# A weight-landing buffer of its own, fewer x and score tiles, and a later gate for block 2's attention

## The chip, the core and the metric

One core of a Trainium2 chip runs the whole program in one launch. Its engines are TensorE (PE, the matmuls), VectorE (DVE), ScalarE (ACT), GpSimd (POOL) and SyncE (SP, which here issues every DMA). The metric is device microseconds of that core. The kernel before took 1076.9 us (median of 3 runs, 1076.82 to 1080.04).

## The reference

Attention over 4 batches of 8 heads, 576 positions and a head width of 64, in which each query keeps its 32 largest scores; then two feed-forward networks (FFNs) over the 2304 resulting rows of 512.

```python
scores = scale * q @ k.T                       # per head, 576 x 576
kth = partition(scores, -32)[..., -32]
scores = where(scores >= kth, scores, -1e9)
attn = softmax(scores); x = attn @ v           # heads side by side: 2304 x 512
h = maximum(x @ moe_w_in, 0); x = h * h @ moe_w_out         # 512 -> 2048 -> 512
h = maximum(x @ w1, x @ w2, x @ w3); out = h @ moe2_w_out   # 512 -> 768 -> 512
```

The weights come in float64 and are turned into float32 on the chip.

## The kernel before, in words

The rows are cut into six blocks of 384 (`units`, last index but one). For each block and each of four pairs of heads, `attend` runs six jobs of 128 queries against all 576 keys of a head. A job is: two matmul groups of 288 columns into PSUM, copied by ScalarE into a score tile `s`; four MAX8 and three MATCH_REPLACE8 on VectorE, which find the 32nd largest score (tiles `w` and `mx`); three ScalarE passes and one GpSimd pass that make the masked exponentials as two fp16 halves; a transposing DMA (`et`); the product with the values on PE; and a normalisation on GpSimd (`xs`, `xg`). The three row tiles of a pair of heads are then transposed on PE and written into the block's x tile (`xt`), as a high half by ScalarE (L507) and a low half by VectorE (L509). One `xt` tile holds a block's x for all four pairs. A matmul of two float32 numbers is three matmuls of such halves.

`moe(g)` is the FFN of block g. It goes through 28 weight chunks: 16 of the first network, nine of w1, w2 and w3, three of the last matrix. `group` (L630) issues every FFN matmul; a product with x is `a<-xt,wt` or `b<-xt,wt`, the last one is `a<-wt,hh`. x is overwritten in place by the first network's result and is read for the last time by the products with w3.

A weight chunk comes as two halves of 512 KB. The first time, a half is converted (`half_chunk`): the raw float64 words are loaded (L588), ScalarE makes the fraction and the exponent from them (`ot<-xt` by `prelu` and `lw<-xt`), VectorE joins the two (L594, the list `joined` keeps these operations), ScalarE and GpSimd make the two halves of the number, and the result is stored in DRAM (`wsc`). From then on the chunk is only reloaded (L576). There are 56 conversions. The first 36 (EARLY, 18 chunks) are begun two at a time with block 0's attention jobs; the other 20, of the last ten chunks, stand in block 0's FFN and write straight to the weight tiles `wt`, of which there are seven.

The raw words land in a spare x tile: `xt` has three slots, the first is given to `spare`, and its 2 x 4 x 384 words are three landing places of 1024. When the last of the 56 conversions has read them, the slot goes to a block's x.

The order of the work is laid out by the kernel itself. `Plan` keeps a list of operations with engines, assumed durations, priorities and dependences, and places them greedily on five engines with a model of time; a buffer can be opened when a slot of its tag is free, and for all tags but `b` in the order in which the buffers were made. The result is a fixed order for each engine. `plan.after` holds an operation back until another one has been placed: at L719 the attention of blocks 2 to 5 is held until `joined[-9]`, the ninth last join, has begun. The FFNs are not held.

Of the kernel before, what the change touches and what calls it, by code (L numbers as in the profile page):

```python
# [11 lines left out]
F32R = mybir.dt.float32r  # L12
F16 = mybir.dt.float16
BF16 = mybir.dt.bfloat16
U32 = mybir.dt.uint32
# [6 lines left out]
P = 128  # L22
# [244 lines left out]
def kernel(ctx, tc, q, k, v, w_in, w_out, w1, w2, w3, w_out2, out):  # L267
# [3 lines left out]
    KD = DM // P  # L271
    NP = H // 2
# [1 line left out]
    ebias = ESHIFT * float(np.log(2.0))  # L274
    eguard = 1e-9 * 2.0 ** ESHIFT

    nbufs = {"ks": 1, "qs": 1, "vst": 2, "kt": 4, "qt": 1, "vt": 4, "vs": 1, "sm": 2, "sc": 2, "us": 6, "s": 6, "w": 2, "e": 3, "e16": 3,
             "et": 3, "mx": 8, "nb": 8, "rc": 4, "xs": 2, "xr": 2, "xg": 3, "xt": 3,
             "hh": 6, "hl": 6, "r": 2, "m0": 1, "m1": 1, "ot": 3, "cw": 2, "lw": 2, "wt": 7,
             "b": 4, "a": 4}  # L280
    spool = ctx.enter_context(tc.tile_pool(name="sb", bufs=1))
# [3 lines left out]
    plan = Plan(nbufs, {"b"})  # L285

    def buf(tag, shape, dtype=F32):
        return Buf(plan, ppool if tag in ("a", "b") else spool, shape, dtype, tag)
# [4 lines left out]
    def act(prio, n, reads, writes, fn, psum=True, ptr=0):  # L293
        plan.op(ACT, c_act(n, psum, ptr), prio, reads, writes, fn)

    def dve(prio, n, reads, writes, fn, rate=1.0, slack=0.0):
        return plan.op(DVE, c_dve(n, rate), prio, reads, writes, fn, slack=slack)

    def gps(prio, n, reads, writes, fn):
        plan.op(POOL, c_pool(n), prio, reads, writes, fn)  # L300
# [4 lines left out]
    def dma(prio, nbytes, reads, writes, fn, ns=650.0):  # L305
        plan.op(SP, ns, prio, reads, writes, fn, lat=max(nbytes / DBW, 90.0))

    def sub(eng, out_ap, a, b):
        eng.tensor_tensor(out_ap, a, b, op=ALU.subtract)  # L309

    def prelu(out_ap, src, slope, **kw):
        return nc.scalar.activation(out_ap, src, AF.Prelu, alpha=slope, **kw)  # L312
# [28 lines left out]
    NW = max(width)  # L341
    EARLY, PER = 18, 2
    XW = max(len(u[1]) for u in units)
    QW = max(len(u[1]) * 2 * P + (3 * D if u[2] else 0) for u in units)
    spare = buf("xt", [P, 2, KD, NW], F32R)
    work = [(spare, x) for x in range(2 * KD * NW // 1024)]
    xt = {}


# [68 lines left out]
    def attend(i, unit, p):  # L418
# [18 lines left out]
        for j, h in jobs:  # L437
            for _ in range(min(PER if g == 0 else 0, len(ahead))):
                half_chunk(False, *ahead.pop(0))
# [104 lines left out]
    joined = []  # L544
# [13 lines left out]
    def weights(g, n):  # L558

        src = chunk_src[n]  # L560
        a, f = src.shape[1], src.shape[2]
        h = a // 2
        wts = [half_chunk(g > 0 or n < EARLY, n, x) for x in range(2)]

        def view(r, kk):
            return wts[kk // h][:, r].rearrange("p (a f) -> p a f", f=f // 2)[:, kk % h]
        return (lambda kk: wts[kk // h]), view

    def half_chunk(again, n, x):

        src = chunk_src[n]
        h, f = src.shape[1] // 2, src.shape[2]
        src = src[:, x * h:(x + 1) * h, :]
        wt, dst = buf("wt" if again or n >= EARLY else "cw", [P, 2, 512], F32R), scratch[n][x]
        if again:
            dma(W_, P * 4096, [dst], [wt], lambda: nc.sync.dma_start(  # L576
                wt[:].rearrange("p a b -> p (a b)").bitcast(F32), dst[:]))
            return wt
        raw = work[(2 * n + x) % len(work)]
        cv = buf("ot", [P, 512])  # L580

        def bits(t=U32):
            return spare[:].rearrange("p x a b -> p (x a b)")[:, 1024 * raw[1]:1024 * raw[1] + 1024].bitcast(t)

        def word(u):
            return bits().rearrange("p (n u) -> p n u", u=2)[:, :, u]

        dma(W_, P * 4096, [], [raw], lambda: nc.sync.dma_start(bits().rearrange("p (a f) -> p a f", f=f), src))  # L588
        act(C_M, 512, [raw], [cv], lambda: prelu(
            cv[:], word(1).bitcast(F32), -2.0 ** 32, scale=2.0 ** -112), psum=False)  # L590
        lw = buf("lw", [P, 512], U32)
        act(C_M, 512, [raw], [lw], lambda: nc.scalar.activation(  # L592
            lw[:], bits(U8).rearrange("p (n u) -> p n u", u=8)[:, :, 3], AF.Copy, scale=1.0 / 32.0, bias=-15.5 / 32.0), psum=False)
        joined.append(dve(C_D, 512, [cv, lw], [cv], lambda: nc.vector.scalar_tensor_tensor(  # L594
            cv[:].bitcast(U32), cv[:].bitcast(U32), 3, lw[:], op0=ALU.logical_shift_left, op1=ALU.bitwise_or),
            rate=1.7, slack=SL / 2))
        act(C_A, 512, [cv], [(wt, 0)], lambda: nc.scalar.copy(wt[:, 0], cv[:]), psum=False)
        gps(C_P, 512, [cv, (wt, 0)], [(wt, 1)], lambda: sub(nc.gpsimd, wt[:, 1], cv[:], wt[:, 0].bitcast(F32)))
        dma(W_, P * 4096, [wt], [dst], lambda: nc.sync.dma_start(
            dst[:], wt[:].rearrange("p a b -> p (a b)").bitcast(F32)))  # L600
        return wt
# [114 lines left out]

    ahead = [(n, x) for n in range(EARLY) for x in range(2)]
    for i in range(NP * len(units)):
        plan.after = joined[-9] if i >= NP * 3 else None  # L719
        u = units[i // NP]  # L720
        attend(i, u, i % NP)
        if i % NP == NP - 1 and (i // NP == len(units) - 1 or units[i // NP + 1][3] != u[3]):
            plan.after = None
            moe(u[3])
# [66 lines left out]
```

## Time and profile before

| | |
|---|---|
| median of 3 runs | 1076.9 us |
| the profiled execution | 1079.8 us |
| its span, first to last instruction | 1078.0 us |
| busy: PE, DVE, ACT, POOL | 984.3, 818.7, 767.8, 625.3 us |
| attention's maxima on DVE end | about 853 us |
| DMA read from HBM, written | 217.25 MB, 34.08 MB |

Busy time is the time in which an engine has an instruction under way. Matmuls overlap one another, so a matmul's own duration is longer than the time it costs in a row of many. A line in a timeline gives the start, the length, the engine, the source line, the operation and its tiles, written "output<-inputs"; in brackets stands how long the engine was idle before it and who ended that. PEclk is the granted clock of PE as a share of full speed. A DMA share of 1 means that all 16 DMA engines have a transfer under way.

### The profile page before, as it was taken

The numbers are of one execution on the slowest core, as the hardware profiler recorded it, in microseconds if no ns is written. First come the engines' busy times: TensorE is split into PE (matmuls) and PEld (weight loads), VectorE is DVE, ScalarE is ACT, GpSimd is POOL, SyncE is SP. The second block draws the span as 40 slices with busy tenths as digits, with TensorE's granted clock in tenths as the row PEclk, the third lists the DMA queues.
The fourth block names the chain that finished last, engine by engine and source line by source line (L and its number), as shares of the span: only waits on it lengthen the run. The fifth ranks groups of instructions, "written<-read, shape, count | busy, mean of one in ns | idle before, by whom it ended". The sixth has DMA issues, their size and how long they took to land.

```text
span 1078.0 us, 18812 instructions
## 1 busy us (share of the span) xinstructions
PE 984.3 (91%) x6116; PEld 889.7 (83%) x6116; DVE 818.7 (76%) x1736; ACT 767.8 (71%) x1616; POOL 625.3 (58%) x887
## 2 busy tenths in 40 slices
PE   5556576999998999999999999999999999999998
PEld 3333343799897899998999998999998999989997
DVE  5999899899976999999999999999999601100020
ACT  6987788899887889976788868888876742123311
POOL 2666677787787577756467676767565641112210
PEclk9999755799999999999999999999999999999999
DMA  9999899999998999999999999999999986787774
GB/s 306 348 308 251 256 285 332 245 269 231 251 341 318 316 348 283 288 288 256 300 261 266 281 284 274 267 237 262 254 256 280 285 261 237 252 266 262 257 239 147
DMA packets 249697, 295.04 MB, mean 274 GB/s; under 512 B 178944, under 2 KB 182528, under 8 KB 249600
## 3 DMA queue, kind: packets, MB, share of 16 engines
q1 hardware_dynamic: 249600, 293.85, 95.1%
q8 instruction: 48, 0.79, 0.3%
q14 instruction: 49, 0.40, 0.1%
HBM read 217.25 MB, written 34.08 MB: 233 GB/s over the span
## 4 chain that ended last, share of the span: by engine, by line
PE 61%; DVE 13%; ACT 11%; POOL 7%; DMA 4%; issue 3%; SPq 0%; POOLq 0%; ACTq 0%; DVEq 0%
PE a L630 37%; PE b L630 13%; DVE mx L452 7%; DVE w L454 6%; PE b L525 5%; PE b L479 4%; DMA xt<-in_moe_w_in_dram 2%; POOL e L309 2%; ACT s L446 1%; ACT e L312 1%; POOL hl L309 1%; DMA xt<-in_moe_w_dram 1%; ACT lw L592 1%; ACT e L460 1%; ACT ot L312 1%
## 5 line engine op out<-in xcount | busy, mean ns | idle before, releaser
L452 DVE MAX8 mx<-w 128x8 f32<-128x576 f32 x432 | 311.1, 746 | 0.1
L309 POOL TENSOR_TENSOR e<-e,e 128x512 f16<-128x512 f32 (+1 forms) x288 | 211.9, 748 | 108.6 <-ACT e L463 91.3
L630 PE MATMUL a<-xt,wt 128*128 128x384 f32 x1296 | 239.3, 339 | 1.0 <-DVE xt L309 0.9
L630 PE MATMUL b<-xt,wt 128*128 128x384 f32 x1152 | 235.9, 346 | 3.5 <-DMA wt<-wsc 1.9
L630 PE MATMUL a<-hh,wt 128*128 128x384 f32 x768 | 228.8, 346 | 0.0
L630 PEld LDWEIGHTS a<-xt,wt 128*128 128x128 f32 x1296 | 224.1, 188 | 2.2 <-DVE xt L309 1.9
L454 DVE MATCH_REPLACE8 w<-mx,w 128x576 f32<-128x576 f32 x288 | 213.1, 742 | 0.0
L630 PEld LDWEIGHTS b<-xt,wt 128*128 128x128 f32 x1152 | 203.8, 192 | 5.8 <-DMA wt<-wsc 1.9
L525 PE MATMUL b<-kt,qt 128*128 128x288 f32 (+1 forms) x640 | 167.9, 395 | 36.2 <-DMA qt<-in_q_dram 17.8
L309 POOL TENSOR_TENSOR hl<-r,hh 128x384 fp32r<-128x384 f32 x96 | 97.3, 1014 | 126.5 <-ACT hh L656 119.2
L525 PEld LDWEIGHTS b<-kt,qt 128*128 128x128 f32 (+1 forms) x640 | 118.1, 218 | 62.5 <-ACT xs L482 16.4
L630 PEld LDWEIGHTS a<-hh,wt 128*128 128x128 f32 x768 | 142.7, 190 | 2.1 <-issue 1.1
L630 PE MATMUL a<-hl,wt 128*128 128x384 f32 x384 | 131.3, 342 | 4.1 <-POOL hl L309 3.8
L312 ACT ACTIVATE e<-s,mx 128x576 f32<-128x576 f32 x144 | 112.2, 779 | 27.7 <-POOL e L309 16.5
L479 PEld LDWEIGHTS <-et 128*128 128x128 f16 (+1 forms) x1440 | 84.1, 108 | 57.6 <-issue 35.4
L446 ACT ACTIVATE s<-b 128x288 f32<-128x288 f32 x288 | 108.0, 409 | 24.8 <-PE b L525 23.2
L479 PE MATMUL b<-vt,et 128*128 128x129 f16 (+3 forms) x1440 | 101.7, 223 | 25.2 <-DMA et<-e 16.8
L460 ACT ACTIVATE e<-e,nb 128x576 f32<-128x576 f32 x144 | 112.1, 779 | 6.8 <-POOL nb L456 4.8
L452 DVE MAX8 mx<-s 128x8 f32<-128x576 f32 x144 | 107.2, 746 | 10.3 <-ACT s L446 10.3
L454 DVE MATCH_REPLACE8 w<-mx,s 128x576 f32<-128x576 f32 x144 | 106.8, 742 | 0.0
L654 ACT ACTIVATE r<-b 128x384 f32<-128x384 f32 x96 | 47.1, 490 | 79.2 <-PE b L630 76.6
L463 ACT CAST e<-e 128x576 f16<-128x576 f32 x144 | 96.6, 672 | 1.6 <-DMA et<-e 1.3
(62 smaller groups left out, 1194.8 us busy)
## 6 DMA issues: line engine op xcount, KB each, us to landing
wt<-wsc SPq DMA_DIRECT2D x316, 512.0 KB, 4.8
wsc<-cw SPq DMA_DIRECT2D x36, 512.0 KB, 4.9
xt<-in_moe_w_out_dram SPq DMA_DIRECT2D x22, 512.0 KB, 6.3
wsc<-wt SPq DMA_DIRECT2D x20, 512.0 KB, 5.7
xt<-in_moe_w_dram SPq DMA_DIRECT2D x18, 512.0 KB, 5.9
xt<-in_moe_w_in_dram SPq DMA_DIRECT2D x16, 512.0 KB, 5.8
ks<-in_k_dram SPq DMA_DIRECT2D x12, 576.0 KB, 5.9
vst<-in_v_dram SPq DMA_DIRECT2D x16, 320.0 KB, 5.8
```

What stands on the lines that cost most here:

```text
L309: eng.tensor_tensor(out_ap, a, b, op=ALU.subtract)
L312: return nc.scalar.activation(out_ap, src, AF.Prelu, alpha=slope, **kw)
L446: act(A_S, HS, [ps], [(s, f)], lambda s=s, cs=cs, ps=ps: nc.scalar.activation(s[:, cs], ps[:, 0:HS], AF.Copy, scale=escale))
L452: dve(A_X, S, [src], [(mx, r)], lambda src=src, mx=mx, m8=m8: nc.vector.max(out=mx[:, m8], in_=src[:]))
L454: dve(A_X, S + 50, [src, (mx, r)], [w_], lambda src=src, mx=mx, m8=m8, w_=w_: nc.vector.match_replace(out=w_[:], in_to_replace=mx[:, m8], ...
L460: act(A_E, S, [e, nb], [e], lambda nb=nb, e=e: nc.scalar.activation(e[:], e[:], AF.Exp, bias=nb[:], scale=-1.0 / KEEP), psum=False, ptr=1)
L463: act(A_E, S, [e], [(e16, 0)], lambda e=e, e16=e16: nc.scalar.copy(e16[:, S:2 * S], e[:]), psum=False)
L479: nc.tensor.matmul(ps[0:m, 0:wv], et[:, mm_, c0:c1], vt[:, hh, vc, 0:wv], start=x == 0, stop=x == 8)
L525: nc.tensor.matmul(ps[:, 0:HS], a, c, start=m == 0, stop=m == len(seq) - 1)
L592: act(C_M, 512, [raw], [lw], lambda: nc.scalar.activation(lw[:], bits(U8).rearrange("p (n u) -> p n u", u=8)[:, :, 3], AF.Copy, scale=1.0 ...
L630: nc.tensor.matmul(o, x, y, start=first and i == 0 and m == 0, stop=last and i == n - 1 and m == 2)
L654: act(MA, N, [ps], [r], lambda r=r, ps=ps: nc.scalar.activation(r[:, 0:N], ps[:, 0:N], AF.Relu))
```

## The change

Raw weights get four tiles `rw` of their own, of 4 KB in each partition, in place of the three places in the spare x tile. `xt` has two slots in place of three. Score tiles `s` go from six to five, `mx` and `nb` from eight to six. The attention of blocks 2 to 5 is held until the fifth last join in place of the ninth last. Nothing that is computed changes.

```diff
-    nbufs = {... "s": 6, ...
-             "et": 3, "mx": 8, "nb": 8, "rc": 4, "xs": 2, "xr": 2, "xg": 3, "xt": 3,
+    nbufs = {... "s": 5, ...
+             "et": 3, "mx": 6, "nb": 6, "rc": 4, "xs": 2, "xr": 2, "xg": 3, "xt": 2, "rw": 4,
...
-    spare = buf("xt", [P, 2, KD, NW], F32R)
-    work = [(spare, x) for x in range(2 * KD * NW // 1024)]
...
-        raw = work[(2 * n + x) % len(work)]
+        raw = buf("rw", [P, 1024], U32)
         cv = buf("ot", [P, 512])
 
         def bits(t=U32):
-            return spare[:].rearrange("p x a b -> p (x a b)")[:, 1024 * raw[1]:1024 * raw[1] + 1024].bitcast(t)
+            return raw[:].bitcast(t)
...
-        plan.after = joined[-9] if i >= NP * 3 else None
+        plan.after = joined[-5] if i >= NP * 3 else None
```

## Rows read from the trace of the kernel before

**Rows 1.** Page: chain that ended last by line; DMA issues (us to landing).

```profile
PE a L630 37%; PE b L630 13%; DVE mx L452 7%; DVE w L454 6%; PE b L525 5%; PE b L479 4%; DMA xt<-in_moe_w_in_dram 2%; POOL e L309 2%; ACT s L446 1%; ACT e L312 1%; POOL hl L309 1%; DMA xt<-in_moe_w_dram 1%; ACT lw L592 1%; ACT e L460 1%; ACT ot L312 1%
...
xt<-in_moe_w_out_dram SPq DMA_DIRECT2D x22, 512.0 KB, 6.3
```

**Rows 2.** Windows, FFN matmuls alone: stretch, PE and weight-load busy (count), clock, DMA.

```profile
292.00:336.00 44.00, 40.05 (x219) 37.52 (x218) 1.00 1.04 339
...
343.90:349.30 5.40, 0.86 (x2) 0.29 (x1) 0.68 0.49 122
349.30:353.00 3.70, 3.67 (x9) 2.95 (x10) 0.54 0.85 343
353.00:360.30 7.30, 6.57 (x27) 4.61 (x26) 1.00 0.98 328
360.30:362.00 1.70, 0.24 (x2) 0.21 (x2) 1.00 0.98 349
```

**Rows 3.** Chain of waits, 325 to 366 us: start, us, what.

```profile
339.07 2.46 ACT s L446 x9
...
344.57 3.04 POOL kt L309
...
355.07 6.67 DMA wt<-wsc
...
361.79 2.37 PE b L630 x12
```

**Rows 4.** Timeline of VectorE, 319 to 354 us: joins and block 2's first maximum.

```profile
319.41 1.37 DVE L594 SCALAR_TENSOR_TENSOR ot<-ot,lw 128x512 uint32<-128x512 uint32 x1 [2.39 <-ACT lw L592]
...
336.67 0.68 DVE L594 SCALAR_TENSOR_TENSOR ot<-ot,lw 128x512 uint32<-128x512 uint32 x1
338.59 0.76 DVE L452 MAX8 mx<-s 128x8 f32<-128x576 f32 x1 [1.24 <-ACT s L446]
...
353.50 1.67 DVE L594 SCALAR_TENSOR_TENSOR ot<-ot,lw 128x512 uint32<-128x512 uint32 x1
```

**Rows 5.** Timeline of SP round 323 us: block 2's query load, a raw load.

```profile
323.25 0.57 SPq L354 DMA_DIRECT2D qs<-in_q_dram  x1
323.91 0.41 SPq L588 DMA_DIRECT2D xt<-in_moe_w_out_dram  x1
```

**Rows 6.** Timelines: last bias of blocks 2 and 5, their x, block 2's FFN.

```profile
471.48 0.29 POOL L456 TENSOR_SCALAR nb<-mx 128x1 f32<-128x1 f32 x1
...
506.77 0.61 DVE L509 SCALAR_TENSOR_TENSOR xt<-b,us,xt 128x384 fp32r<-128x384 f32 x1
...
514.64 0.69 PE L630 MATMUL b<-xt,wt 128*128 128x384 f32 x3
...
855.56 0.29 POOL L456 TENSOR_SCALAR nb<-mx 128x1 f32<-128x1 f32 x1
...
886.18 0.62 DVE L509 SCALAR_TENSOR_TENSOR xt<-b,us,xt 128x384 fp32r<-128x384 f32 x1 [2.34 <-ACT xt L507]
```

**Rows 7.** Timeline of ScalarE at 334 us: block 2's query cast.

```profile
334.00 0.84 ACT L413 CAST qt<-qs 128x768 fp32r<-128x768 f32 x1
```

**Rows 8.** Waits of the whole span: who, for whom, us, times, longest.

```profile
ACT ot L312 <- POOL cw L309: 9.8, 10, 1.9
```

**Rows 9.** Windows, all engines: PE, PEld, DVE, ACT, POOL busy, clock, DMA share, GB/s.

```profile
300.00:325.00 25.00, 24.62 (x159) 23.79 (x158) 18.32 (x29) 21.20 (x42) 23.52 (x27) 1.00 1.07 346
```

**Rows 10.** Timeline of ScalarE at 795 us: block 5's first x.

```profile
795.62 0.58 ACT L507 ACTIVATE xt<-b,us 128x384 fp32r<-128x384 f32 x1
```

**Rows 11.** Tile xt on PE, 780 to 832 us: durations ns, first and last start.

```profile
L630 PE MATMUL a<-xt,wt x153: 331/336/423, 780.2 to 813.8; 128*128 128x384 f32 x153
```

**Rows 12.** Chain of waits, whole span: PE begins block 5's FFN.

```profile
956.05 4.21 PE b L630 x24
```

**Rows 13.** Timelines at 744 us: a score tile's last reader, the next first maximum.

```profile
743.10 0.79 ACT L312 ACTIVATE e<-s,mx 128x576 f32<-128x576 f32 x1
...
744.88 0.74 DVE L452 MAX8 mx<-s 128x8 f32<-128x576 f32 x1
```

More of the change, by code (lines that the diff above doesn't have):

```diff
@@ L275 @@
     eguard = 1e-9 * 2.0 ** ESHIFT
-    nbufs = {"ks": 1, "qs": 1, "vst": 2, "kt": 4, "qt": 1, "vt": 4, "vs": 1, "sm": 2, "sc": 2, "us": 6, "s": 6, "w": 2, "e": 3, "e16": 3,
-             "et": 3, "mx": 8, "nb": 8, "rc": 4, "xs": 2, "xr": 2, "xg": 3, "xt": 3,
+    nbufs = {"ks": 1, "qs": 1, "vst": 2, "kt": 4, "qt": 1, "vt": 4, "vs": 1, "sm": 2, "sc": 2, "us": 6, "s": 5, "w": 2, "e": 3, "e16": 3,
+             "et": 3, "mx": 6, "nb": 6, "rc": 4, "xs": 2, "xr": 2, "xg": 3, "xt": 2, "rw": 4,
              "hh": 6, "hl": 6, "r": 2, "m0": 1, "m1": 1, "ot": 3, "cw": 2, "lw": 2, "wt": 7,
```

## The prediction, made before the result

> **What bounds the kernel now.** I read the page's chain of waits first: of the chain that ended last, TensorE (PE) on the FFN line L630 has 37% and 13% of the span, and no other line has more than 7% [rows 1]. So a microsecond moves the end only if PE gains or loses it. I then looked for stretches in which PE lacks work after the first block. The table of FFN matmuls by stretch shows one cluster [rows 2]. From 292 to 336 us PE does 219 matmuls in 44 us, 0.18 us each with little else beside them, so it is full. From 343.9 to 349.3 us it does 2. From 349.3 to 353 us it does 9 while the granted clock is 0.54, so nearly all of it at the 1.2 GHz level. From 353 us it does 27 512-wide ones in 6.57 us, 0.23 to 0.24 each. After 360.3 us it has nothing until 361.79 us [rows 2, 3].
>
> The chain of waits inside this hole says why [rows 3]. ScalarE copies scores of block 2 for 2.46 us, GpSimd makes a kt tile of block 2 for 3.04 us, and only then come the last weight halves that block 0's FFN waits for. The second piece is the first reload of block 1's weights: 6.67 us from its issue at 355.07 us to the first matmul at 361.79 us. That issue waits for the last of the 56 conversions, because weight tiles are handed out in a fixed order.
>
> What the hole costs: 5.40 us less two matmuls of 0.23 is 4.9; 3.70 us less nine of 0.23 is 1.6; 361.79 less 360.3 is 1.5. Together 8.0 us, the most that can be won here.
>
> **The change, part by part.** *The wait of block 2.* Nine joins start from 319.41 to 353.50 us on VectorE [rows 4]. The query load of block 2 leaves SP at 323.25 us [rows 5], just behind the ninth last join; VectorE's first maximum of block 2 is at 338.59 us [rows 4], 19.2 us after that join. With the fifth last join as the gate, all of block 2's work (query, key and value loads, casts on ScalarE, kt and qt on GpSimd, scores on PE, and the maxima) is planned after 336.67 us or its new place. It therefore leaves ScalarE and GpSimd free for the last four halves, which today it delays.
>
> When is the fifth last join now? Its raw load leaves SP at 323.91 us [rows 5], 0.66 us behind the query load, once the third landing buffer is free. With a fourth buffer it can leave one conversion earlier, about 3 us, so I put the join at 333.7 us (bounds 331 and 336.7). The last raw load then waits for the buffer of the fifth last half, not the fourth last: issue about 333.5, 6.3 us to landing [rows 1], two ScalarE passes and the join: about 344 us. Today the reload leaves 1.6 us after the last join's start (355.07 less 353.50). So it would leave near 345.5 and land by 352.2 us. PE's last FFN product, 54 matmuls of 0.23 us from 336 us on, ends at about 348.5 us. Of the 8.0 us, up to 3.7 stay as a wait for the reload, and some of them are filled by block 2's scores. I take a gain of **5.0 us**. Bounds: 8.0, and 3.0 if the last four joins keep today's pace of 16.8 us (333.7 + 16.8 + 1.6 + 6.7 = 358.8, 3.0 before 361.8).
>
> *What is late next.* Block 2's attention starts later, and behind it stands the FFN of block 2. VectorE does block 2's jobs back to back after 338.59 us; the last job's bias is at 471.48 us, its x is written from 506.77 to 507.4 us, and PE starts on that x at 514.64 us [rows 6]. The slack is 7.2 us. Of the 19.2 us from gate to first maximum, ScalarE took the query cast only at 334.00 us [rows 7] although the load left at 323.25 us and needs about 6; some 4.6 us of that are conversions in its way. So 14.6 us with them gone: first maximum at 333.7 + 14.6 = 348.3, a delay of 9.7 us (bounds 7 from 331 + 14.6, and 17.3 from 336.67 + 19.2). Four joins of 0.7 us no longer stand between block 2's maxima, which gives back 2.8. The lag from last bias to x is 35.9 us here and 31.2 us in the last block (855.56 to 886.80) [rows 6]; where PE waits for it I take 4 us off. So x is ready at 507.4 + 9.7 - 2.8 - 4 = 510.3 us, against PE being done at 514.64 - 5.0 = 509.6 us. That costs **0.5 us** (bounds 0 and 8.6, below).
>
> *Four landing tiles.* Before 290 us a further buffer buys nothing: ScalarE's first pass already idles for GpSimd's last step on an earlier half [rows 8], so the joined tile is the scarce one there. From 292 to 336 us PE is full, so an earlier conversion is hidden under its matmuls. Value 0 there, its whole worth is in the 3 us above; without that cover it would be worth a few us, and against it stands one more load in a busy queue, 0 to 1.5 us.
>
> A rule speaks against this part. Between 300 and 325 us the DMA engines move 346 GB/s and their share is 1.07 [rows 9]: the queue is full when the extra load would go in. The Trainium skill (DMA: Bandwidth & Descriptors, Queues, rings and completion order) says that an engine takes its descriptors in ring order; so a raw load put ahead of the query load is paid by the query. 0.52 MB at 346 GB/s are 1.5 us, and with them the cost at block 2 would be 2.0 us in place of 0.5, the gain 3.0 in place of 4.5. The sum here leaves it out, since the query is gated behind the load that moves anyway.
>
> *Two x tiles.* Block n+2 writes x only once block n's last product with x is done. Block 5 writes its first x at 795.62 us [rows 10], and block 3 reads its x until 813.8 us [rows 11]: an 18 us wait. Three xg tiles stand ahead of it, and even a shift of the whole block by 18 us puts its x at 905 us against 956.05 us, when PE starts block 5 [rows 6, 12]. Value 0, bounds 0 and a few tenths where PE's order changes.
>
> *Five score tiles, six mx and nb.* In the tightest place that I found, the tile of the fifth job back is released at 743.89 us and the next first maximum is at 744.88 us [rows 13]; a score needs about 2 us from there, so VectorE would lose about 1 us now and then, far behind in time of what PE waits for. Value 0; the bound is 1 us in block 2, where the lead is over 10 us.
>
> **Sum.** -5.0 + 0.5 = -4.5 us. The profiled execution took 1079.8 us (span 1078.0 and 1.8 around it), so it would take 1075.3 us. It lies 2.9 us above the median of the runs shown, 1076.9; from there **1072.4 us**.
>
> **The rivals.** *The hole only moves.* Block 2's first maximum comes about 13 us later (half way between my value and the bound). x is then ready at 515.6 (2 us taken off the lag), PE at 509.6; 6 us, of which one partial product of 1.6 us (nine matmuls that do without the last pair of heads) is filled. -5.0 + 4.4 = -0.6: 1076.3 us. For: the slack is only 7.2 us. Against: the lag can shrink when PE is idle.
>
> *The gate is too late (slower).* One mechanism: the gate join stays at 336.67 us, the path behind it keeps its 19.2 us, and PE runs out of work before block 2's FFN near 512 us. x at 507.4 + 17.3 - 2.8 = 521.9, PE ready at 511.6 with the gain of 3.0; two partial products fill 3.3 us; idle 7.0 and, as after the hole at 343.9, 1.6 us at the lower clock level: 8.6. -3.0 + 8.6 = +5.6: 1082.5 us. It decides from a delay of about 13 us, a first maximum at 352 us. For: from 300 us on the path shares one full DMA queue with the conversions. Against: with the conversions ahead of it, it is alone.
>
> *The whole hole goes and nothing follows*: -8.0, 1069 us. For: no later block is as tight. Against: the reload still needs its 6.67 us.
>
> *Two x tiles hold the last block up*: slower from a delay of 69 us (956.05 less 886.80) on; at 18 us it is free. Its price beyond that is one to one; I set 1083 us.
>
> **How the numbers follow.** Forecast 0.50, the hole only moves 0.20, gate too late 0.20, whole hole gone 0.06, x tiles 0.04. What a measurement of this kernel can tell from no change is about 0.3%, 3.2 us, so faster means under 1073.7 us. The forecast lies only 1.3 us inside that: I count 0.40 of its 0.50 as faster and 0.10 as the same. The moved hole gives 0.16 same and 0.02 to each side. Faster 0.40 + 0.06 + 0.02 = 0.48; same 0.26; slower 0.26. The instruction order of every engine is laid out anew, and a few us either way come with that; so the range goes from 1064 (the whole hole and 5 more) to 1084 us (the late gate and 1.5 more). The forecast's own range is 1069 to 1076.
>
> **What would show it.** Right: no stretch of 5 us between 336 and 365 us in which PE does two FFN matmuls; block 1's first product before 356 us; the last join before 348 us; block 2's first maximum between 345 and 352 us; PE going from block 1 to block 2 near 510 us without a gap of over 2 us and with the clock at its upper level; scores and maxima of later blocks as dense as now. Wrong: the last join still near 353 us (the conversions were not held up by attention); or a gap with a lower clock between 500 and 525 us ahead of the first product of block 2 (late gate); or a gap of PE after 830 us that ends on x (two x tiles).

## The result: slower by 0.6%

The changed kernel takes 1084.2 us (median of 10 runs, 1080.2 to 1089.8) where the kernel before takes 1076.9 us (10 runs, 1074.7 to 1081.6): a ratio of 1.0060, interval 1.0037 to 1.0084. Forecast were 1072.4 us and faster. The two profiled executions took 1082.5 and 1079.8 us: they show 2.7 of the 7.3 us, as the one of before lies 2.9 us above its median and the one of after 1.7 us below.

### The profile page after: what moved, and what is told of

The parts are those of the page before. It is cut to its first block, busy times and chain, and to the rows that moved or that the text cites. A ratio compares the mean times of both kernels' runs of the same rounds, so it can differ in the third digit from the quotient of the medians.

```text
span 1080.7 us, 18818 instructions
## 1 busy us (share of the span) xinstructions
PE 975.4 (90%) x6116; PEld 886.1 (82%) x6116; DVE 819.5 (76%) x1736; ACT 765.3 (71%) x1616; POOL 624.0 (58%) x887
## 4 chain that ended last, share of the span: by engine, by line
PE 73%; ACT 7%; POOL 4%; DVE 4%; issue 3%; DMA 0%; POOLq 0%; ACTq 0%
PE a L628 44%; PE b L628 17%; PE b L523 7%; PE b L477 5%; DVE mx L450 2%; DVE w L452 1%; POOL e L309 1%; ACT s L444 1%; ACT e L458 1%; POOL hl L309 1%; POOL wt L309 1%; ACT e L312 1%; PE b L503 1%; DVE ot L592 1%; ACT lw L590 1%
## 5 line engine op out<-in xcount | busy, mean ns | idle before, releaser
L309 POOL TENSOR_TENSOR e<-e,e 128x512 f16<-128x512 f32 (+1 forms) x288 | 214.1, 755 | 82.0 <-ACT e L461 61.7
L628 PE MATMUL a<-xt,wt 128*128 128x384 f32 x1296 | 242.2, 341 | 0.7 <-DVE xt L309 0.7
L523 PE MATMUL b<-kt,qt 128*128 128x288 f32 (+1 forms) x640 | 162.7, 386 | 32.1 <-DMA qt<-in_q_dram 13.6
L523 PEld LDWEIGHTS b<-kt,qt 128*128 128x128 f32 (+1 forms) x640 | 115.7, 213 | 58.0 <-ACT s L444 14.9
```

The lines of the kernel that those rows point to most:

```text
L523: nc.tensor.matmul(ps[:, 0:HS], a, c, start=m == 0, stop=m == len(seq) - 1)
L628: nc.tensor.matmul(o, x, y, start=first and i == 0 and m == 0, stop=last and i == n - 1 and m == 2)
```

## The profile after

The page: the chain that ended last by line. Lines are two lower than before.

```profile
PE a L628 44%; PE b L628 17%; PE b L523 7%; PE b L477 5%; DVE mx L450 2%; DVE w L452 1%; POOL e L309 1%; ACT s L444 1%; ACT e L458 1%; POOL hl L309 1%; POOL wt L309 1%; ACT e L312 1%; PE b L503 1%; DVE ot L592 1%; ACT lw L590 1%
```

PE on the FFN line now holds 61% of the chain where it held 50% [rows 1]; it is still what a microsecond must be won from. The windows of FFN matmuls that answer to [rows 2]:

```profile
292.00:336.00 44.00, 38.55 (x204) 36.60 (x205) 0.96 1.06 316
...
343.90:349.30 5.40, 4.43 (x20) 3.42 (x19) 1.00 0.82 318
```

The stretch of 5.4 us with two matmuls has 20, and the clock stays at its upper level. But the stretch ahead of it, full before with 219, has 204. The same count over the whole first half says how gain and loss stand. First the kernel before (stretch, PE and weight loads with their counts, clock, DMA):

```profile
0.00:200.00 200.00, 12.18 (x30) 8.41 (x30) 0.81 0.99 296
200.00:225.00 25.00, 18.68 (x87) 16.62 (x87) 0.88 0.98 235
225.00:336.00 111.00, 92.79 (x484) 83.41 (x485) 1.00 1.00 285
336.00:362.00 26.00, 16.03 (x56) 11.13 (x56) 0.87 0.84 303
362.00:515.00 153.00, 129.78 (x657) 113.17 (x656) 1.00 1.06 295
```

Then the changed one:

```profile
0.00:200.00 200.00, 9.81 (x24) 7.01 (x24) 0.74 0.97 285
200.00:225.00 25.00, 16.62 (x89) 15.31 (x90) 1.00 1.08 333
225.00:336.00 111.00, 90.63 (x466) 81.25 (x466) 0.98 1.02 277
336.00:362.00 26.00, 21.28 (x97) 16.83 (x96) 1.00 0.95 346
362.00:515.00 153.00, 127.31 (x638) 111.33 (x636) 0.99 1.02 287
```

Up to 336 us it is 22 matmuls behind (579 against 601), some 4 us at 0.18 us each. In the hole it does 41 more. From 362 to 515 us it does 19 fewer. At 515 us the two are level, 1314 each: the hole was won, and lost ahead of it and behind it. The 2.7 us by which this execution ends later come after that, and most of them inside block 4's FFN: it begins at 829.4 us in both, block 5's 2.2 us later than before (PE, before and after):

```profile
955.88 4.88 PE L630 MATMUL b<-xt,wt 128*128 128x384 f32 x27
```

```profile
958.05 4.87 PE L628 MATMUL b<-xt,wt 128*128 128x384 f32 x27
```

One place behind the hole is at 433.6 us, where PE waits for a low half whose sources stand behind a cast of keys for block 3 and a score copy on ScalarE (the chain of waits there: start, us, what):

```profile
428.19 1.04 ACT kt L363
...
431.11 0.30 ACT s L444
...
432.55 1.01 POOL hl L309
433.55 0.04 issue
433.60 0.62 PE a L628 x2
```

The rows that answer to [rows 4 to 7], out of the timelines of VectorE, SP and ScalarE, and then of GpSimd, PE and VectorE later on:

```profile
332.05 0.70 DVE L592 SCALAR_TENSOR_TENSOR ot<-ot,lw 128x512 uint32<-128x512 uint32 x1 [1.63 <-ACT lw L590]
348.19 0.69 DVE L592 SCALAR_TENSOR_TENSOR ot<-ot,lw 128x512 uint32<-128x512 uint32 x1 [0.49 <-ACT lw L590]
356.13 1.42 DVE L450 MAX8 mx<-s 128x8 f32<-128x576 f32 x2 [1.12 <-ACT s L444]
...
333.40 0.48 SPq L352 DMA_DIRECT2D qs<-in_q_dram  x1
...
348.66 0.83 ACT L411 CAST qt<-qs 128x768 fp32r<-128x768 f32 x1
```

```profile
484.37 0.29 POOL L454 TENSOR_SCALAR nb<-mx 128x1 f32<-128x1 f32 x1
...
515.60 1.66 PE L628 MATMUL b<-xt,wt 128*128 128x384 f32 x8
516.16 0.62 DVE L507 SCALAR_TENSOR_TENSOR xt<-b,us,xt 128x384 fp32r<-128x384 f32 x1
...
896.75 0.62 DVE L507 SCALAR_TENSOR_TENSOR xt<-b,us,xt 128x384 fp32r<-128x384 f32 x1 [2.53 <-ACT xt L505]
```

The fifth last join is at 332.05 us and the last at 348.19 us. The query load leaves at 333.40 us, but ScalarE takes its cast only at 348.66 us, behind all the conversions; block 2's first maximum is at 356.13 us, 24.1 us behind the gate and 17.5 us later than before.

## The experiments

Each ran in five rounds beside the kernel before. The ratio to it is given, because its median moved between 1076.9 and 1080.1 us from one set of runs to the next.

**Which part.** Two theories: the gate is too late (block 2), or the score tiles are too few (front).

```diff
before_gate5:   kernel before,  joined[-9] -> joined[-5]
after_gate9:    kernel after,   joined[-5] -> joined[-9]
before_score5:  kernel before,  "s": 6 -> 5, "mx": 8 -> 6, "nb": 8 -> 6
after_score6:   kernel after,   "s": 5 -> 6, "mx", "nb": 6 -> 8, "rw": 4 -> 3
```

> The kernel before with only the wait of block 2's attention moved from the ninth to the fifth last join; all buffers as before. Late gate (the wait is the cause): block 2's first maximum at 352 to 356 us and a time of 1081 to 1085 us, slower than before by about what the whole change costs (7 us). Score tiles (five of them, and six of mx and nb, are the cause): the hole round 344 us shrinks and nothing is lost ahead of it, 1071 to 1075 us. Landing tiles are the cause: the same, 1071 to 1076 us. As theories on the parts give opposite signs here, this run is the first cut.

> The changed kernel with only the wait put back to the ninth last join; landing, x and score tiles as changed. Late gate: within 2 us of the kernel before, 1075 to 1079 us, with block 2's first maximum near 340 us. Score tiles: the attention of block 0 still ends about 8 us later (x of its last pair of heads near 195 us instead of 187), the hole of 336 to 362 us is back, and the time is 1083 to 1089 us. Landing tiles: also 1082 to 1088 us, told apart from the score tiles by the next run.

> The kernel before with only five score tiles and six mx and nb. Score tiles: the scores of block 0 are written later, x of its last pair of heads comes at 192 to 197 us instead of 187, TensorE loses 2 to 4 us more before 200 us and 2 to 3 us more round 320 us, 1080 to 1084 us. Late gate or landing tiles: x of the last pair at 187 to 189 us, time within 1.5 us of the kernel before.

> The changed kernel with six score tiles and eight mx and nb as before, and three landing tiles of their own instead of four (which is the room that this takes); two x tiles and the wait for the fifth last join stay. Score tiles: block 0's x of the last pair back at 187 to 189 us, the hole smaller than before, 1072 to 1076 us. Late gate: 1081 to 1085 us, with block 2's first maximum at 352 us or later. The two together: about half way, 1077 to 1080 us.

| run | us | ratio, interval |
|---|---|---|
| before_gate5 | 1077.1 | 0.9990, 0.9973 to 1.0006 |
| after_gate9 | 1089.4 | 1.0099, 1.0071 to 1.0127 |
| before_score5 | 1089.9 | 1.0103, 1.0077 to 1.0130 |
| after_score6 | 1076.6 | 0.9989, 0.9972 to 1.0005 |

The late gate fell as the cause of the loss: alone it costs nothing that the runs can tell (0.9990). Both kernels with five score tiles and the ninth last join are 1% slower, after_gate9 just above what was expected. Three landing tiles of their own and two x tiles are worth nothing: after_score6 has them and before_gate5 has not, 0.9989 and 0.9990, and by their traces PE's order is the same in both up to 792 us. The fourth landing tile, and six mx and nb with six score tiles, have no run of their own. But my account of how five tiles cost was wrong: x of block 0's last pair came at 189.4 us (before: 187.0; expected 192 to 197), and the loss was larger than expected.

before_gate5 tests the gate's terms by themselves. Its windows of FFN matmuls, then rows of its timeline (VectorE, PE):

```profile
0.00:355.20 355.20, 137.42 (x655) 118.04 (x656) 0.89 0.99 291
336.00:362.00 26.00, 19.23 (x80) 13.71 (x78) 1.00 0.99 356
505.00:520.00 15.00, 8.77 (x39) 6.87 (x39) 0.89 1.01 260
510.00:515.00 5.00, 2.03 (x6) 1.48 (x7) 0.71 0.79 226
```

```profile
348.25 1.42 DVE L452 MAX8 mx<-s 128x8 f32<-128x576 f32 x2 [1.27 <-ACT s L446]
...
352.37 0.67 DVE L594 SCALAR_TENSOR_TENSOR ot<-ot,lw 128x512 uint32<-128x512 uint32 x1
...
504.04 1.30 PE L630 MATMUL b<-xt,wt 128*128 128x384 f32 x6
...
511.08 0.60 DVE L509 SCALAR_TENSOR_TENSOR xt<-b,us,xt 128x384 fp32r<-128x384 f32 x1
...
515.08 0.52 PE L630 MATMUL a<-hh,wt 128*128 128x384 f32 x1
```

In the hole 80 matmuls stand where 56 stood. A block's FFN has 654 of them; the 655th begins at 355.2 us, where before it began at 361.79 us [rows 3]. So PE leads by 6.6 us after the hole (0.5 us of it from ahead of the hole), and by 10.6 us when it starts block 2 (504.04 us, before 514.64 us [rows 6]). There it runs short: x comes only at 511.08 us, 39 matmuls are done from 505 to 520 us, and the clock is at 0.71 for a part of it. The kernel before has there, and as its first product with block 2's `hh`:

```profile
505.00:520.00 15.00, 12.63 (x55) 9.52 (x54) 1.00 1.10 298
```

```profile
520.31 0.42 PE L630 MATMUL a<-hh,wt 128*128 128x384 f32 x1
```

At that product the lead is 5.2 us, and 3.1 us when block 2 has done 110 matmuls (535.1 us, before 538.2 us). Of 10.6 us, 7.5 are given back at this one hand-over.

**Order or tile.** Five tiles act twice: an instruction waits for a free tile, and the planner, which knows the number, lays out another order. The next run has the order for five tiles (in the traces the same on every engine as before_score5) and six tiles to run in. The two after it hold one score tile back for a part of the time and keep eight mx and nb. Even so five_front has the order of before_score5 up to about 360 us: up to there, six mx and nb add nothing to what five score tiles do to the order. five_later has the order of the kernel before up to about 340 us. The last run moves a constant of the planner.

```diff
order5_tiles6:  before_score5, and the place in memory apart from the planner's count:
-                b.slot = x[1]
+                b.slot = heads[k] % {"s": 6, "mx": 8, "nb": 8}[k[1]] if k[1] in ("s", "mx", "nb") else x[1]
five_front:     kernel before, a tile of "s" taken from the first to the last raw load
+    held = buf("s", [P, S])
+        dma(W_, P * 4096, [held], [raw], ...
five_later:     kernel before, a tile of "s" taken from block 2's first load to the end
jitter_hp:      kernel before
-HP = 1.4
+HP = 1.45
```

> The kernel before whose order is laid out for five score tiles (and six mx and nb), instruction for instruction that of the run with five score tiles, but the tiles of the memory are six (and eight): only the waits for a free tile go. If the wait for a tile costs the 11 us of that run, most of it comes back: 1077 to 1081 us. If the order that five tiles force costs it, the time stays at 1087 to 1091 us.

> The kernel before with one of its six score tiles held back until the last raw weight load, near 330 us: five score tiles for blocks 0 and 1, six after that; its order is that of the run with five score tiles up to about 330 us. There TensorE had lost 5.4 us more than before up to 325 us, and 3.6 us less in the hole behind it. If the front alone pays: 1085 to 1090 us. If the loss is spread over front and later blocks: 1079 to 1083 us, and the cost of this run and the next one add up to about 11 us. If the front is made up for by the hole: 1077 to 1079 us.

> The kernel before with one of its six score tiles held back from block 2's attention to the end: six for blocks 0 and 1, five after that; its order is that of the kernel before up to about 330 us. If only the front pays: within 1.5 us of the kernel before. If the loss is spread: 1082 to 1087 us, with more of TensorE's waits for the hidden low half (hl) of GpSimd in blocks 2 to 5.

> The kernel before, all tiles and the wait as before, with one constant of the planner's time model (the factor on a hop between engines) at 1.45 instead of 1.40: the order is laid out anew for no reason of the work. If a greedy order that is laid out anew is worth several us by chance, 1070 to 1074 or 1082 us and more; if the score tile is the cause as such, within 3 us of the kernel before.

| run | us | ratio, interval |
|---|---|---|
| order5_tiles6 | 1088.9 | 1.0086, 1.0066 to 1.0106 |
| five_front | 1086.7 | 1.0063, 1.0045 to 1.0081 |
| five_later | 1081.9 | 1.0018, 1.0004 to 1.0033 |
| jitter_hp | 1084.1 | 1.0051, 1.0033 to 1.0069 |

The order costs it: without the waits for a tile 1.0086 of 1.0103 is still there, and the intervals do not tell the 0.17% between them from nothing. By five_front and five_later most of it comes with the order of blocks 0 and 1 (0.63% against 0.18%), but the order of five_front behind 360 us is a new one as well, and five_later lies between what its two theories gave. And jitter_hp upset the theory of score tiles: with all six, and no reason in the work at all, a new order cost 0.51%.

**Five tiles, or any new order.**

```diff
six_hop220:   kernel before,  HOP = 180.0 -> 220.0
six_hp135:    kernel before,  HP = 1.4 -> 1.35
five_hp145:   kernel before,  "s": 6 -> 5, HP = 1.4 -> 1.45
five_hp135:   kernel before,  "s": 6 -> 5, HP = 1.4 -> 1.35
after_hp135:  kernel after,   HP = 1.4 -> 1.35
after_hp145:  kernel after,   HP = 1.4 -> 1.45
```

> The kernel before with the planner's time for taking over a freed tile at 220 instead of 180 ns, and nothing else: an order laid out anew with six score tiles. If an order laid out anew costs a few us whatever the tiles (the order of the kernel before is one of the better ones), 0.2 to 0.8% above the kernel before. If the first such run (a hop factor of 1.45, 0.5% slower) was an exception: within 0.2%.

> The kernel before with the planner's hop factor at 1.35 instead of 1.40: a second order laid out anew with six score tiles. Expected as for the run with 220 ns: 0.2 to 0.8% above the kernel before if any new order costs that, within 0.2% if not.

> The kernel before with five score tiles and the hop factor at 1.45. If five tiles as such force a worse order: 0.8 to 1.5% above the kernel before, that is 0.5% or more above the run with six tiles and the same factor. If the loss of the run with five tiles was an unlucky order: 0 to 0.7%, overlapping the runs with six.

> The kernel before with five score tiles and the hop factor at 1.35. As for the factor 1.45: 0.8 to 1.5% above the kernel before if five tiles force a worse order, 0 to 0.7% if it was an unlucky one.

> The changed kernel, all its tiles and its wait, with the planner's hop factor at 1.35 instead of 1.40. If the change is slower because its five score tiles got an unlucky order: it may land anywhere from 0.5% below to 0.8% above the kernel before, and away from the changed kernel's 0.6% by more than 0.3%. If the parts of the change as such cost the time: 0.4 to 0.8% above.

> The changed kernel with the hop factor at 1.45. As for 1.35: anywhere from 0.5% below to 0.8% above the kernel before if the order is what decides; 0.4 to 0.8% above if the parts of the change do.

| new order by | six tiles | five tiles | the changed kernel |
|---|---|---|---|
| factor 1.40 | (before) | 1.0103 | 1.0060 |
| factor 1.45 | 1.0051 | 1.0090 (1.0070 to 1.0109) | 1.0019 (1.0004 to 1.0034) |
| factor 1.35 | 1.0056 (1.0036 to 1.0076) | 1.0006 (0.9993 to 1.0018) | 1.0014 (1.0000 to 1.0029) |
| take-over 220 ns | 1.0033 (1.0016 to 1.0050) | not run | not run |

The 1.0103 is before_score5, with six mx and nb; the two below it have eight, so only they differ in the constant alone. It moves the kernel with five tiles by 0.8%, from 1.0090 to 1.0006, and the changed kernel from 1.0060 to 1.0014. So the 0.6% is not the price of the change's parts as such. six_hop220 and six_hp135 came as expected if any new order costs something; five_hp145 came as expected if five tiles force a worse order, five_hp135 as expected if the order was an unlucky one. Three orders with six tiles average 0.47% above the kernel before, three with five 0.66%: with such a spread this does not show that five tiles cost anything as such.

**One place of the order.** In before_score5 PE loses most between 200 and 225 us: 61 FFN matmuls against 87. Its FFN window there, then two rows of the timeline:

```profile
200.00:225.00 25.00, 12.95 (x61) 11.33 (x60) 0.80 0.73 187
```

```profile
209.43 2.97 PE L525 MATMUL b<-kt,qt 64*128 64x288 f32 x6 [2.33 <-ACT xs L482]
...
207.47 0.78 ACT L460 ACTIVATE e<-e,nb 128x576 f32<-128x576 f32 x1 [1.87 <-POOL nb L456]
```

ScalarE waits for a bias, with the copies that free PE's buffers behind it. The run moves those two copies ahead and changes nothing else in the order.

```diff
five_swap:  before_score5, two copies (L482) ahead of one exponential and its cast (L460, L463)
```

> The kernel before with five score tiles, in the same order but for one place on ScalarE near 207 us: the exponential of a job and its cast (lines 460 and 463) go behind the two copies of the product with the values (line 482) instead of ahead of them. In the run with five tiles ScalarE waits there 1.87 us for the bias of that job, TensorE then 2.33 us for the copies, and TensorE's clock is at its lower level from 209.5 to 219.5 us. If such places of the order carry the cost: the gap and the low clock behind it go, TensorE loses about 6 us instead of 11.0 us between 200 and 225 us, and the kernel takes 1083 to 1087 us, 0.3 to 0.5% less than with five tiles alone. If TensorE was short of work there anyway: unchanged at 1.0% above the kernel before.

It took 1088.3 us, 1.0101 (1.0076 to 1.0126): as before_score5. The same window, and PE (one line further down in this kernel):

```profile
200.00:225.00 25.00, 15.21 (x70) 13.29 (x68) 0.86 0.80 196
```

```profile
207.62 0.75 PE L526 MATMUL b<-kt,qt 64*128 64x288 f32 x2 [1.25 <-ACT s L447]
209.49 3.10 PE L526 MATMUL b<-kt,qt 64*128 64x288 f32 x8 [0.40 <-ACT s L447]
```

The wait for the copies went, and a shorter one for scores came in its place; nine matmuls were won there, about 1.6 us, too little to be told apart in the time. The 0.3 to 0.5% did not come back: this place does not hold the loss. No other place was tried.

**Other gates.**

```diff
six_gate7:       after_score6, joined[-5] -> joined[-7]
split_gate:      kernel before, the DMAs of the attention held for joined[-9], its work for joined[-5]
-            o.soft.add(self.after)
+            o.soft.add(self.after[eng == SP])
split_gate_rw3:  the same split in after_score6
```

> Six score tiles, eight mx and nb, three landing tiles of their own, two x tiles, and the wait at the seventh last join, between the ninth and the fifth. The hole of 336 to 362 us costs between 8 and 3 us and block 2 comes between 3 and 10 us later: if the two trade evenly, 1075 to 1079 us, as with the ninth and the fifth; if a middle gate is better than both, 1071 to 1074 us.

> The kernel before, all its tiles, with the wait split: block 2's DMAs (and all others of the attention of blocks 2 to 5) are held for the ninth last join as before, its work on the four engines for the fifth last. In the run with the fifth for both, the hole gave TensorE 5.0 us back and block 2's first maximum came at 348.3 us, after which TensorE lost 4.3 us more than before between 425 and 600 us. If the loads' 6 us on the way are what makes block 2 late: first maximum near 343 us, hole closed as far, 1074 to 1076 us, 0.2 to 0.4% below the kernel before. If the earlier work of block 2 pushes the last conversions back again: the hole is back, and the time is within 0.2% of the kernel before. An order laid out anew from 320 us on may add 0 to 0.5% by itself.

> The same split wait with three landing tiles of their own, two x tiles, six score tiles and eight mx and nb. As split_gate by either theory, within 0.2% of it, unless the order round the last conversions comes out otherwise.

They took 1086.6 us (1.0086, 1.0056 to 1.0115), 1086.2 us (1.0060, 1.0036 to 1.0084) and 1087.9 us (1.0074, 1.0052 to 1.0097). six_gate7 is above what either theory gave. So is split_gate, unless the 0.5% that its expectation allowed for a new order is counted in; its hole is back (first line below), as its second theory said, though block 2's first maximum came at 343.4 us, as its first one said. split_gate_rw3 is within 0.2% of it, as expected. In six_gate7 the hole came back, 51 FFN matmuls where before has 56, and ScalarE's timeline shows why:

```profile
336.00:362.00 26.00, 15.31 (x52) 11.19 (x51) 0.80 0.76 264
```

```profile
336.00:362.00 26.00, 14.05 (x51) 10.07 (x50) 0.87 0.75 273
```

```profile
344.48 0.62 ACT L595 CAST wt<-ot 128x512 fp32r<-128x512 f32 x1 [2.80 <-DVE ot L592]
...
346.38 4.74 ACT L444 ACTIVATE s<-b 128x288 f32<-128x288 f32 x12
351.01 0.67 ACT L312 ACTIVATE ot<-rw 128x512 f32<-128x512 f32 x1
```

In six_gate7 twelve score copies of block 2 stand ahead of the last conversions, as nine did in [rows 3]. Where they fall is again the order's doing. Of all that ran, none beats the kernel before by more than its interval.

## Why the prediction was wrong

*The step that failed* is "Five score tiles, six mx and nb ... Value 0; the bound is 1 us". It was read from the times at which tiles come free, and for that it holds as far as the runs can tell: the waits are not what costs (order5_tiles6). But the number of tiles also enters the planner, which lays out every engine's order anew from the first score on. before_score5 measured that at 11 us, order5_tiles6 at 9; in the changed kernel the whole came to 7.3 us, and it was gone in after_score6, with six score tiles, eight mx and nb and three landing tiles. The prediction did name a new order, as "a few us either way", but for the range alone; in the sum it stood at nothing. Its size was about right. As an even bet it was wrong: over the 19 kernels that ran here (the changed one and 18 more) the middle ratio is 1.0060 and the lowest 0.9989, which is not told from 1. These are not 19 separate draws: in six of them (before_gate5, after_score6, five_later, six_gate7 and the two split gates) PE's order is that of the kernel before up to about 337 us, and before_score5, order5_tiles6 and five_swap have one order but for one place. But the three with six tiles and only a constant moved are all slower, by 0.33 to 0.56%. Why the order of the kernel before is among the best was not looked into; a choice of its constants by time is one possibility. The loss of the changed kernel's order is its own: with another constant it is 0.14 to 0.19% above before. What in an order makes it slow stays open. PE's waits for `hl` from 190 us on are one candidate, before and in before_score5 (us, times, longest):

```profile
PE a L630 <- POOL hl L309: 3.8, 6, 1.1
```

```profile
PE a L630 <- POOL hl L309: 8.0, 12, 1.7
```

But these waits do not follow the time from run to run: in six_gate7, whose profiled span is 1091.0 us, they are 4.4 us, and in jitter_hp, with 1079.2 us, 8.9 us:

```profile
PE a L628 <- POOL hl L309: 4.4, 8, 1.1
```

```profile
PE a L630 <- POOL hl L309: 8.9, 9, 2.4
```

So they are not the cause by themselves, and mending one place did not bring the time back.

*The hole*, 8.0 us with a gain of 5.0: right in its mechanism. Alone the gate won 6.1 us there. In the changed kernel the joins ended at 348.19 us (said: near 344) and PE did 41 matmuls more; but PE came to the last products of block 0 4.6 us late (340.59 us, before 336.00 us), so that block 1 began at 358.92 us, only 2.9 us earlier than before. One reading of [rows 3] was wrong: the kt tile of 344.57 us is not block 2's. The keys of its batch were made between 154 and 216 us, and this tile is the first of block 3. It stands behind the gate all the same.

*The fifth last join* at 333.7: measured 332.05, within its bounds. before_gate5 has it at 334.58 us without a fourth landing tile, so some 2 us of the 4.6 needed no fourth tile. Whether one raw load more makes block 2's query late, the point that spoke against the tile, was not tested: the query's cast stood behind the conversions in ScalarE's order.

*The delay of block 2.* Alone the gate put the first maximum at 348.25 us (said 348.3) and x at 511.08 (said 510.3). In part that is luck: the last join was to come ahead of block 2, near 344 us, and came behind its first maximum, at 352.37 us. The cost was 7.5 us and not 0.5 (510.3 less 509.6 is 0.7, besides), because PE reached block 2 at 504.04 us and not at 509.6: it led by 6.6 us behind the hole and won 4.0 more on the way. Block 2's own scores and products, which lie beside block 1's FFN, came later too and left PE a part of that room: between 362 and 480 us they keep it busy for 26.9 us, before 28.1 us. PE is also idle for 1.5 us less there; the rest is open. The outcome is that of the rival "the hole only moves", 0.6 us faster by its sum and 1.3 measured, not told from nothing. In the changed kernel the delay was 17.5 us, past the point of the rival "gate too late". Its gap did not come: PE, late itself, ended block 1 at 515 us and x was there at 516.16. So the slower side came out by a mechanism that no rival had. Of the signs of being right, the last join (before 348 us), block 1's first product (before 356) and the first maximum (345 to 352) missed; none of the signs of being wrong came.

*Landing tiles, two x tiles*: 0, right for three landing tiles (0.9989 beside 0.9990); the fourth was not timed by itself. Block 5's x comes 10.6 us later, 896.75 us, far ahead of PE.

## What to carry to other kernels

Where a program lays out the order from buffer counts and assumed durations, changing a count is two changes: price the second by laying the order out a few times with a constant moved that means nothing, and time those. A change is a gain only if it stands out from that spread, here 1%. And a wait that is removed ahead of a full engine can come back at the next hand-over, as in before_gate5, if the work behind it was delayed by more than that hand-over's slack.

## What the runs showed of the hardware

A join on VectorE takes 0.66 to 0.70 us in 30 of its 56 places in the kernel before, and as often in six_gate7. In six_gate7 one takes 4.39 us, while GpSimd runs three operations back to back:

```profile
340.06 4.39 DVE L592 SCALAR_TENSOR_TENSOR ot<-ot,lw 128x512 uint32<-128x512 uint32 x1 [1.08 <-ACT lw L590]
...
339.84 1.30 POOL L309 TENSOR_TENSOR wt<-ot,wt 128x512 fp32r<-128x512 f32 x1
341.09 1.02 POOL L309 TENSOR_TENSOR hl<-m,hh 128x384 fp32r<-128x384 f32 x1
342.06 1.84 POOL L309 TENSOR_TENSOR qt<-qs,qt 128x768 fp32r<-128x768 f32 x1
```

It ends 0.55 us after the last of them, and ScalarE's cast of that half waits 2.80 us for it. The Trainium skill (SBUF — State Buffer, SBUF: two separate sides) says that a VectorE operation with two SBUF inputs and a GpSimd operation share a pair of ports that one of them holds for its whole instruction. The trace agrees, and shows besides that GpSimd can keep the join out over three operations in a row. It is no single case: in after_hp135 a join takes 4.56 us, from 308.82 us on, and ends at 313.38 us, 0.56 us after the last of four such operations in a row (312.82 us). The joins of 1.37 and 1.67 us in [rows 4] also end 0.55 us after a GpSimd operation (320.23 and 354.62 us). That the ports are the reason was not tested by a run.
